# Sums of two MLPs: an accumulating DMA in place of VectorE's adds in the middle blocks

## The chip, the cores and the metric

The kernel runs on one core of a Trainium2 chip. The metric is the device time of one execution in microseconds, here a median of three runs. The core has five engines with a queue of instructions each: TensorE (PE in the rows, its weight loads PEld), VectorE (DVE), ScalarE (ACT), GpSimd (POOL) and SyncE (SP). They wait for each other by semaphores. DMAs are issued from the queues of SP, ACT or POOL.

## The reference

The input is a decaying linear attention over 2 sequences of 768 tokens with 8 heads of 64, followed by two MLPs without residuals, all in float32:

```
x = attention(q, k, v, lam)                       # 1536 tokens x 512
h = x @ w_in          # 512 x 2048
x = (h * clip(h + 3, 0, 6) / 6) @ w_out           # first MLP, 2048 x 512
h = x @ w_in2
out = maximum(0.01 * h, h) @ w_out2               # second MLP
```

The attention goes block by block of 64 tokens, with a state of 64 x 64 per head that decays from block to block.

## The kernel before

The kernel has three stages that overlap at their borders. The attention takes about the first 50 us. Then the two MLPs follow. Every float32 operand of a large product is split into a high and a low part, and a product is taken as three matmuls (high by high, high by low, low by high). TensorE does them in groups of 128 x 512 outputs.

The 2048 hidden units are cut into 16 slices of 128, called f. The 1536 tokens are cut into three tiles of 512, called t. A step is one (f, t): a first-stage product (`gemm1`, 12 matmuls into PSUM), a gate on ScalarE and VectorE that ends in G, and a second-stage product (`gemm2`) of four groups e = 0 to 3, three matmuls each, one PSUM bank per group. The slices are taken in blocks (`BLOCKS`, line 30: 1, 3, 4, 4, 4 slices in the first MLP and four times 4 in the second). Within a block, tile by tile, the groups of all its slices accumulate in PSUM; at the end of a block and tile the four accumulators are added to `sums` in SBUF (`SUM[t][:, e, :]`) and their banks are free for the next tile. In the second MLP the first-stage products of tiles 0 and 1 are taken together by a Strassen scheme (`product`, `keep`, `join`) at two places of each block; tile 2 uses `gemm1`.

The banks are `acc0` to `acc3`. In the first MLP the groups e = 0 and 1 of tile 1 use banks of the pool `a` (`acc_bank`, line 505), so e = 2 and e = 3 always come back to the same banks.

`collect` (line 527) empties an accumulator. In the first block of an MLP (b = 0) ScalarE copies it to `sums`; in every other block VectorE adds it to `sums`. `second` (line 631) registers the four groups of a step and, in the last step of a block and tile, their collects.

Weights come as 64-bit floats in halves of 512 KB, by DMA from SP into a ring of four `raw` buffers (`sizes`, line 120). ScalarE and VectorE convert each half (two activations, two tensor_scalar instructions, two that compose the bits) and split it into high and low parts in a ring of six slots `w`. A raw buffer is free when its bits are composed; in the second MLP one raw buffer of each pair of slices is reused for Strassen's sums of weights and is held longer.

The order of all instructions on every engine is written out ahead by a planner, the class `Order`. Each operation has an engine and a duration, a due time, the operations that it follows, and buffers that it takes and gives back. `issue` runs through a simulated time: whenever an engine is idle, the ready operation with the earliest due time whose buffers are free starts on it, and at that moment its instructions are emitted. The chip then runs each engine's instructions strictly in this order, with waits by semaphores. In the plan a VectorE collect lasts 0.69 us and a ScalarE collect 0.58 us; a bank is given back when the collect ends. The second-stage groups keep their order among themselves (`prev2`), so do the first-stage products (`prev1`).

Of the kernel before, what the change touches and what calls it, by code (L numbers as in the profile page):

```python
# [9 lines left out]
F32 = mybir.dt.float32  # L10
# [4 lines left out]
ALU = mybir.AluOpType  # L15
# [8 lines left out]
P = 128  # L24
TT = 512
# [4 lines left out]
BLOCKS = ((1, 3, 4, 4, 4), (4, 4, 4, 4))  # L30
# [5 lines left out]
T_FIRST, T_STEP, T_COLLECT, HOP = 40.0, 5.45, 2.0, 0.3  # L36
# [6 lines left out]
class Order:  # L43
# [7 lines left out]
    def add(self, engines, fn, due=1e9, after=(), takes=(), frees=()):  # L51


        engines = [engines] if isinstance(engines, tuple) else engines
        self.ops.append((engines, fn, due, [a for a in after if a is not None], list(takes), list(frees)))
        return len(self.ops) - 1
# [59 lines left out]
def decay_attention_two_mlps(ctx: ExitStack, tc: tile.TileContext, qkk, vv, lam, w1, w2, out):  # L116
    nc = tc.nc
    eng = {"act": nc.scalar, "dve": nc.vector, "pool": nc.gpsimd}

    sizes = {"raw": 4, "cv": 3, "cl": 2, "w": 6, "G": 3, "u": 3, "h": 2, "a": 2, "r": 3, "vs": 3}  # L120
    late = {"s": 2, "Gx": 3, "ux": 3}
    const = ctx.enter_context(tc.tile_pool(name="const", bufs=1))
    sb_att = ExitStack()
    pool = {n: (sb_att if n in ("r", "vs") else ctx).enter_context(
                tc.tile_pool(name=n, bufs=sizes[n], **({"space": PSUM} if n in "ha" else {})))
            for n in sizes}
# [5 lines left out]
    add = od.add  # L132

    def new(n, shape, dtype, name=None):
        return pool[n].tile(shape, dtype, tag=name or n, name=name or n)
# [3 lines left out]
    steps = [(l, b, t, f) for l in range(2) for b in range(len(BLOCKS[l])) for t in range(NTT)  # L139
             for f in range(starts[l][b], starts[l][b + 1])]  # L140
# [9 lines left out]
    due2 = [d + 1.5 * T_STEP for d in due1]  # L150
# [14 lines left out]
    SUM = [sums[:, t * KC * TT:(t + 1) * KC * TT].rearrange("p (k n) -> p k n", k=KC) for t in range(NTT)]  # L165
# [99 lines left out]
    def scores(c):  # L265
        def fn(_):

            ps, qk = PA["s", c], QK[c % NQ]
            for h in range(H):
                for b in range(2):  # L270
                    nc.tensor.matmul(ps[own[b], b, h, :], qk[other[b], 1, h, :], qk[other[b], 0, h, :],  # L271
                                     start=True, stop=True)
        return fn
# [54 lines left out]
    st, copies, masks, dense_ops, att_ops = {}, {-1: []}, [], [op_warm], []  # L328
    for c in range(NSC):
        d, last = due_c[c], c + 1 == NSC  # L330
        ks = [] if last else [add(("pool", 1.05), k_decay(c, b), d,
                                  after=[ld["qk", c], op_const, st.get(c - 2)]) for b in (1, 0)]
        pe = ("pe", 1.15)
        qc = add(("act", 1.2) if c else ("none", 0.0), queries(c), d - 0.5, after=[ld["qk", c]], takes=["pair"])
        s = add(pe, scores(c), d, after=[qc, op_warm])
# [5 lines left out]
        if not last:  # L341
            st[c] = add(pe, state(c), d + 1.3, after=ks + [ld["v", c]] + copies[c - 1] + ([op_rows[c % 2]] if c else []),
                        takes=["a"])
# [30 lines left out]
    def low_bits(h):  # L374
        def fn(_):

            CV[h] = [new("cv", [P, DM], U32, "t"), new("cl", [P, DM], U32, "c")]
            nc.scalar.activation(out=CV[h][1], in_=RAW[h][:, :, 0], func=AF.Copy, scale=2.0 ** -29)  # L378
        return fn
# [15 lines left out]
    def compose(h):  # L395
        def fn(_):
            t, c = CV[h]

            nc.vector.scalar_tensor_tensor(out=t, in0=RAW[h][:, :, 1], scalar=0xC0000000, in1=t,  # L399
                                           op0=ALU.bitwise_and, op1=ALU.bitwise_or)  # L400
            nc.vector.tensor_tensor(out=t, in0=t, in1=c, op=ALU.add)  # L401
        return fn
# [37 lines left out]
    for l in range(2):  # L440
        for f in range(NF):
            for j in range(2):
                h = (l, f, j)
                held = l == 1 and j == 0
                ld_w = add(("dma", 1.45), load_w(h), takes=["raw"])
                a = add(("act", 0.67), low_bits(h), after=[ld_w], takes=["cv", "cl"])
                m = add(("act", 0.67), magnitude(h), after=[ld_w, a])
                x = add(("dve", 0.85), exponent(h), after=[m])
                c = add(("dve", 1.4), compose(h), after=[a, x], frees=["cl"] + ["raw"] * (not (held and f % 2)))
# [13 lines left out]
    PH, U, G, ACC = {}, {}, {}, {}  # L463
# [41 lines left out]
    def acc_bank(s, e):  # L505
        return "a" if e < 2 and steps[s][2] % 2 and not steps[s][0] else f"acc{e}"

    def gemm2(s, e):
        def fn(_):
            l, b, t, f = steps[s]  # L510
            wh, wl = W[l, f]
            gh, gl = G[s]
            first, last = f == starts[l][b], f + 1 == starts[l][b + 1]
            if first:
                n = acc_bank(s, e)
                ACC[e] = new("a", [P, TT], F32) if n == "a" else pool["acc"].tile([P, TT], F32, tag=n, name=n)
            es = slice(e * P, (e + 1) * P)
            if l == 0:
                terms = ((wh[:, 1, es], gh), (wh[:, 1, es], gl), (wl[:, 1, es], gh))
            else:  # L520
                terms = ((gh[:, es], wh[:, 1]), (gh[:, es], wl[:, 1]), (gl[:, es], wh[:, 1]))
            for n, (a, x) in enumerate(terms):
                nc.tensor.matmul(ACC[e], a, x, start=(first and n == 0), stop=(last and n == 2))  # L523
            PA["acc", s, e] = ACC[e]
        return fn

    def collect(s, e):
        def fn(x):
            l, b, t, f = steps[s]
            ps, acc = PA["acc", s, e], SUM[t][:, e, :]  # L530
            if b:
                nc.vector.tensor_tensor(out=acc, in0=ps, in1=acc, op=ALU.add)  # L532
            else:
                nc.scalar.copy(out=acc, in_=ps)
        return fn
# [10 lines left out]
    def store(t, e):  # L546
        c0 = (t * SPT + e) * C

        def fn(_):

            for b in range(B):
                queue = nc.scalar if b and t == NTT - 1 else nc.sync
                queue.dma_start(out=out[b * S + c0:b * S + c0 + C, :], in_=SUM[t][own[b], e, :])
        return fn
# [73 lines left out]
    x2_ready, taken, prev1, prev2, sums_of, last1 = {}, {}, None, None, {}, {}  # L628
    gates = {}

    def second(s, gl, w_frees):
        nonlocal prev2
        l, b, t, f = steps[s]
        first, last = f == starts[l][b], f + 1 == starts[l][b + 1]
        sums = []
        for e in range(4):
            bank = acc_bank(s, e)
            prev2 = add(("pe", 0.68), gemm2(s, e), due2[s], after=[gl, w_ready[l, f, 1], prev2],
                        takes=[bank] if first else [], frees=([] if e < 3 else w_frees))
            if not last:  # L640
                continue
            c = add(("dve", 0.69) if b else ("act", 0.58), collect(s, e), due2[s] + T_COLLECT,
                    after=[prev2, *taken.get((t, e), [])], frees=[bank])
            sums.append(c)
            taken[t, e] = [c]
            if l == 1 and b + 1 == len(BLOCKS[l]):
                add(("dma", 0.75), store(t, e), due2[s], after=[c])
        return sums
# [12 lines left out]
    b = len(BLOCKS[1]) - 1  # L661
    due_p["2", b, 2, NF - 2], due_p["2", b, 2, NF - 1] = at, at + 2.72
    for s in range(n0, NS):
        l, b, t, f = steps[s]
        due1[s], due2[s] = due_p["1", f], due_p["2", b, t, f]

    for s in range(n0):
        l, b, t, f = steps[s]
        last = f + 1 == starts[l][b + 1]
        xs = [x_ready[c] for c in range(t * SPT, (t + 1) * SPT)]  # L670
        g1 = add(("pe", 2.73), gemm1(s), due1[s], after=[w_ready[l, f, 0], prev1] + xs, takes=["h", "G"])
        prev1 = g1
        ua = add(("act", 0.69), gate_a(s), after=[g1], takes=["u"])
        gb = add(("dve", 0.69), gate_b(s), after=[ua], frees=["h"])
        gh = add(("act", 0.63), g_high(s), after=[gb])
        gl = add(("dve", 0.69), g_low(s), after=[gh], frees=["u"])
        sums = second(s, gl, ["G"] + ["w"] * (t == NTT - 1))
        if last and b + 1 == len(BLOCKS[l]):
            sums_of[t], last1[t] = sums, g1
# [30 lines left out]
    for p in range(NF // 2):  # L710
# [19 lines left out]
        for f, t, i, c in ((f1, PAIR[0], 0, c11), (f1, PAIR[1], 3, c12), (f2, PAIR[1], 1, c22)):  # L730
            s, n = s_at[f, t], "G" if t == PAIR[0] else "Gx"
# [4 lines left out]
        s = s_at[f2, PAIR[0]]  # L736
        src = PH[s] = lambda p=p: PA["S", p, 0]
        ua = add(("act", 0.6), (lambda s, src: lambda _: (PH.__setitem__(s, src()), leak(s, None)(_)))(s, src),
                 after=[p4], takes=["u"])
# [4 lines left out]
    for f in range(NF):  # L744
        s = next(s for s in range(n0, NS) if steps[s][2:] == (2, f))
        g1 = add(("pe", 2.73), gemm1(s), due1[s], after=[w_ready[1, f, 0], prev1, split[2, 0], split[2, 2]],
                 takes=["a"])
# [4 lines left out]
    for s in range(n0, NS):  # L752
        gl, n = gate[s]
        second(s, gl, [n] + ["w"] * (steps[s][2] == NTT - 1))
# [40 lines left out]
```

## Time and profile before

| | before |
|---|---|
| median of 3 runs | 575.12 us (573.12 to 575.61) |
| profiled execution | 573.51 us |
| its span | 571.3 us |
| TensorE busy | 557.7 us (98%) |
| VectorE busy | 414.0 us (72%) |
| ScalarE busy | 304.0 us (53%) |
| POOL busy | 28.3 us (5%) |
| mean granted TensorE clock | 0.995 of full |

The span goes from the first to the last instruction of the profiled execution; what lies around it is 2.2 us. A busy time is the sum of an engine's instructions; matmuls overlap by their pipelining, so TensorE's busy time says that it is never without one, not that it is at its peak. A granted clock of 1.00 is 2.4 GHz, one of 0.50 is 1.2 GHz.

### The profile page before, as it was taken

To read this page: it belongs to the slowest core of one execution; us is meant where nothing else is said; L and a number is where in the kernel's file an instruction comes from. 1 tells how busy PE (TensorE), PEld (TensorE's weight loads), DVE (VectorE), ACT (ScalarE), POOL (GpSimd) and SP (SyncE) were. 2 spreads that over 40 slices of the span, in tenths; PEclk is the share of its full clock that TensorE was granted. 3 is DMA by queue.
4 is the path that set the end of the run, shared out by engine and by line. 5 is a ranking of instruction groups with operands and counts; after the bars stand their busy time and mean duration, and the time that the engine had idled before them with its cause. 6 is when DMAs were issued, how large, how long until landed. Compare 5 with 4: busy or idle time off the path is not lost.

```text
span 571.3 us, 8498 instructions
## 1 busy us (share of the span) xinstructions
PE 557.7 (98%) x3396; PEld 462.1 (81%) x3396; DVE 414.0 (72%) x676; ACT 304.0 (53%) x510; POOL 28.3 (5%) x33
## 2 busy tenths in 40 slices
PE   8888999999999999999999999999999999999996
PEld 5877888888888888888888888888888888888885
DVE  8678889998848972698879898479864987653222
ACT  5687875557227532564536667477435653443110
POOL 6561000000000000000000000000000000000000
PEclk9899999999999999999999999999999999999999
DMA  8892333224303230012120114213221121000332
GB/s 332 325 357 99 111 110 111 97 87 149 110 1 108 77 110 1 17 57 74 75 74 1 37 38 141 81 38 111 73 75 37 38 74 38 0 1 1 75 73 73
DMA packets 14536, 49.81 MB, mean 87 GB/s; under 512 B 1698, under 2 KB 1698, under 8 KB 14498
## 3 DMA queue, kind: packets, MB, share of 16 engines
q1 hardware_dynamic: 14176, 48.77, 25.3%
q8 instruction: 26, 0.43, 0.3%
q10 hardware_dynamic: 322, 0.52, 0.3%
q14 instruction: 12, 0.10, 0.1%
HBM read 46.14 MB, written 3.15 MB: 86 GB/s over the span
## 4 chain that ended last, share of the span: by engine, by line
PE 91%; DVE 0%; issue 0%
PE acc L523 42%; PE h L475 23%; PE h L602 11%; PE a L475 8%; PE a L523 4%; PE a L602 2%; PE h L308 1%; PE a L296 1%; DVE sums L532 0%; PE pair L271 0%
## 5 line engine op out<-in xcount | busy, mean ns | idle before, releaser
L482 ACT ACTIVATE u<-h,three 128x512 f32<-128x512 f32 x48 | 33.1, 690 | 79.8 <-PE h L475 79.4
L475 PE MATMUL h<-xh,wh 128*128 128x512 f32 x192 | 74.9, 390 | 0.0
L475 PE MATMUL h<-xl,wh 128*128 128x512 f32 x192 | 74.7, 389 | 0.0
L475 PE MATMUL h<-xh,wl 128*128 128x512 f32 x192 | 74.7, 389 | 0.0
L532 DVE TENSOR_TENSOR sums<-acc,sums 128x512 f32<-128x512 f32 x76 | 50.7, 688 | 19.8 <-PE acc L523 19.8
L523 PE MATMUL acc<-Gh,wh 128*128 128x512 f32 x160 | 62.3, 390 | 0.0
L523 PE MATMUL acc<-Gh,wl 128*128 128x512 f32 x160 | 62.3, 389 | 0.0
L523 PE MATMUL acc<-Gl,wh 128*128 128x512 f32 x160 | 62.2, 389 | 0.0
L486 DVE SCALAR_TENSOR_TENSOR u<-u,h 128x512 f32<-128x512 f32 x48 | 32.9, 685 | 26.8 <-ACT u L482 26.7
L409 ACT CAST wh<-t 128x512 fp32r<-128x512 f32 x64 | 38.9, 618 | 24.2 <-DVE t L401 14.5
L523 PE MATMUL acc<-wh,Gh 128*128 128x512 f32 x128 | 49.8, 389 | 0.0
L523 PE MATMUL acc<-wl,Gh 128*128 128x512 f32 x128 | 49.8, 389 | 0.0
L523 PE MATMUL acc<-wh,Gl 128*128 128x512 f32 x128 | 49.8, 389 | 0.0
L401 DVE CUSTOM_DVE_ANT_0 t<-t,c 128x1024 uint16<-128x1024 uint16 x64 | 45.0, 703 | 2.2
L413 DVE TENSOR_TENSOR wl<-t,wh 128x512 fp32r<-128x512 f32 x64 | 42.9, 686 | 4.0 <-ACT wh L409 3.8
L399 DVE SCALAR_TENSOR_TENSOR t<-raw,t 128x512 uint32<-128x512 uint32 x64 | 44.7, 698 | 1.3
L378 ACT ACTIVATE c<-raw 128x512 uint32<-128x512 uint32 x64 | 42.6, 668 | 5.6 <-DVE t L401 4.6
L382 ACT ACTIVATE t<-raw 128x512 f32<-128x512 f32 x64 | 42.5, 664 | 5.0 <-DVE wl L413 5.0
L502 DVE TENSOR_TENSOR Gl<-u,Gh 128x512 fp32r<-128x512 f32 x24 | 16.6, 690 | 39.1 <-ACT Gh L619 39.0
L475 PEld LDWEIGHTS h<-xh,wh 128*128 128x128 f32 x192 | 36.0, 188 | 7.5
L475 PEld LDWEIGHTS h<-xl,wh 128*128 128x128 f32 x192 | 36.0, 188 | 7.5
L475 PEld LDWEIGHTS h<-xh,wl 128*128 128x128 f32 x192 | 36.0, 188 | 7.5
(128 smaller groups left out, 1120.6 us busy)
## 6 DMA issues: line engine op xcount, KB each, us to landing
raw<-w SPq DMA_DIRECT2D x64, 512.0 KB, 3.3
sums<-qkk SPq DMA_DIRECT2D x12, 768.0 KB, 6.8
vs<-vv SPq DMA_DIRECT2D x6, 512.0 KB, 5.4
out<-sums SPq DMA_DIRECT2D x20, 128.0 KB, 2.3
out<-sums ACTq DMA_DIRECT2D x4, 128.0 KB, 3.3
lam_sb<-lam ACTq DMA_DIRECT2D x1, 0.0 KB
```

What stands on the lines that cost most here:

```text
L378: nc.scalar.activation(out=CV[h][1], in_=RAW[h][:, :, 0], func=AF.Copy, scale=2.0 ** -29)
L382: return lambda _: nc.scalar.activation(out=CV[h][0].bitcast(F32), in_=RAW[h][:, :, 1].bitcast(F32), func=AF.Abs)
L399: nc.vector.scalar_tensor_tensor(out=t, in0=RAW[h][:, :, 1], scalar=0xC0000000, in1=t, op0=ALU.bitwise_and, op1=ALU.bitwise_or)
L401: nc.vector.tensor_tensor(out=t, in0=t, in1=c, op=ALU.add)
L409: nc.scalar.copy(out=cut(*h, 0), in_=CV[h][0].bitcast(F32))
L413: return lambda e: eng[e].tensor_tensor(out=cut(*h, 1), in0=CV[h][0].bitcast(F32), in1=cut(*h, 0).bitcast(F32), op=ALU.subtract)
L475: nc.tensor.matmul(ps, a[:, 0, ws], x[:, k, :], start=(n == 0), stop=(n == 3 * KC - 1))
L482: nc.scalar.activation(out=U[s], in_=PH[s], func=AF.Relu, bias=three, scale=1.0)
L486: return lambda _: nc.vector.scalar_tensor_tensor(out=U[s], in0=U[s], scalar=6.0, in1=PH[s], op0=ALU.min, op1=ALU.mult)
L523: nc.tensor.matmul(ACC[e], a, x, start=(first and n == 0), stop=(last and n == 2))
L532: nc.vector.tensor_tensor(out=acc, in0=ps, in1=acc, op=ALU.add)
L602: nc.tensor.matmul(ps, ws[a][:, k * P:(k + 1) * P], xs[b][:, k], start=(i < 3 and n == 0), stop=(n == 5), skip_group_check=True)
```

## The change

In the blocks of an MLP that are neither its first nor its last (`by_dma`), ScalarE copies an accumulator into a staging buffer of a new ring `st` of two buffers, each 128 x 512 float32 (256 KB in all). A DMA issued from POOL with `accum_op=add` then adds the staging buffer to `sums`. The bank is given back when the copy ends; the staging buffer when the DMA ends. For the planner the copy takes 0.58 us of ScalarE and the DMA 3.0 us of POOL. The ring `raw` goes from four buffers to three. The first block's copies and the last block's adds stay as they are.

```diff
-    sizes = {"raw": 4, "cv": 3, "cl": 2, "w": 6, ...}
+    sizes = {"raw": 3, "st": 2, "cv": 3, "cl": 2, "w": 6, ...}
...
+    STAGE = {}
+    by_dma = lambda s: 0 < steps[s][1] < len(BLOCKS[steps[s][0]]) - 1
+
+    def add_up(s, e):
+        t = steps[s][2]
+        return lambda _: nc.gpsimd.dma_start(out=SUM[t][:, e, :], in_=STAGE[t, e], accum_op=ALU.add)
+
     def collect(s, e):
         def fn(x):
             l, b, t, f = steps[s]
             ps, acc = PA["acc", s, e], SUM[t][:, e, :]
-            if b:
+            if by_dma(s):
+                STAGE[t, e] = new("st", [P, TT], F32)
+                nc.scalar.copy(out=STAGE[t, e], in_=ps)
+            elif b:
                 nc.vector.tensor_tensor(out=acc, in0=ps, in1=acc, op=ALU.add)
             else:
                 nc.scalar.copy(out=acc, in_=ps)
...
-            c = add(("dve", 0.69) if b else ("act", 0.58), collect(s, e), due2[s] + T_COLLECT,
-                    after=[prev2, *taken.get((t, e), [])], frees=[bank])
+            far = by_dma(s)
+            c = add(("dve", 0.69) if b and not far else ("act", 0.58), collect(s, e), due2[s] + T_COLLECT,
+                    after=[prev2, *(taken.get((t, e), []) if not far else [])], frees=[bank], takes=["st"] * far)
+            if far:
+                c = add(("pool", 3.0), add_up(s, e), due2[s] + T_COLLECT, after=[c, *taken.get((t, e), [])],
+                        frees=["st"])
             sums.append(c)
             taken[t, e] = [c]
```

## Rows read from the trace of the kernel before

**Rows 1.** The page, parts 1 and 4: busy us and share; chain by engine.
```profile
PE 557.7 (98%) x3396; PEld 462.1 (81%) x3396; DVE 414.0 (72%) x676; ACT 304.0 (53%) x510; POOL 28.3 (5%) x33
...
PE 91%; DVE 0%; issue 0%
```

**Rows 2.** Windows: busy us of PE, PEld, DVE, ACT, POOL; PEclk, DMA share.
```profile
0.00:50.00 50.00, 41.43 (x984) 34.82 (x985) 39.81 (x54) 34.02 (x59) 28.27 (x33) 0.97 0.82 307
50.00:560.00 510.00, 510.00 (x2387) 422.39 (x2386) 370.78 (x618) 269.46 (x452) 0.00 (x0) 1.00 0.20 66
560.00:571.30 11.30, 6.24 (x28) 4.84 (x26) 3.42 (x5) 0.56 (x2) 0.00 (x0) 0.89 0.29 93
```

**Rows 3.** Groups by line and form, the collects: busy us, mean ns.
```profile
L532 DVE TENSOR_TENSOR sums<-acc,sums 128x512 f32<-128x512 f32 x76 | 50.7, 688 | 19.8 <-PE acc L523 19.8
...
L534 ACT COPY sums<-acc 128x512 f32<-128x512 f32 x22 | 12.7, 589 | 0.8
```

**Rows 4.** Chain in order of time, first MLP: start us, us, what.
```profile
87.52 2.72 PE acc L523 x12
90.24 2.72 PE h L475 x12
92.96 1.36 PE a L523 x6
94.32 1.36 PE acc L523 x6
...
188.16 5.44 PE acc L523 x24
```

**Rows 5.** Timeline of TensorE, second MLP: start us, us, line, op, out<-in.
```profile
409.68 0.39 PE L523 MATMUL acc<-wh,Gh 128*128 128x512 f32 x1
...
410.13 0.39 PE L523 MATMUL acc<-wh,Gl 128*128 128x512 f32 x1
...
415.12 0.39 PE L523 MATMUL acc<-wh,Gxh 128*128 128x512 f32 x1
```

**Rows 6.** Timeline of VectorE at the same end of a block.
```profile
409.20 2.73 DVE L532 TENSOR_TENSOR sums<-acc,sums 128x512 f32<-128x512 f32 x4 [0.23 <-PE acc L523]
```

**Rows 7.** Timelines of ScalarE and VectorE and the chain: one gate.
```profile
148.84 0.63 ACT L492 ACTIVATE Gh<-u 128x512 fp32r<-128x512 f32 x1 [0.25 <-DVE u L486]
...
150.65 0.68 DVE L499 SCALAR_TENSOR_TENSOR Gl<-u,Gh 128x512 fp32r<-128x512 f32 x1
...
152.80 1.36 PE a L523 x6
```

**Rows 8.** The page, part 6: issues by queue, KB each, median us to landing.
```profile
raw<-w SPq DMA_DIRECT2D x64, 512.0 KB, 3.3
...
out<-sums SPq DMA_DIRECT2D x20, 128.0 KB, 2.3
```

**Rows 9.** Tiles raw (all, then from 130 us) and out: issue ns, landing us.
```profile
L371 SPq DMA_DIRECT2D raw<-w x64: 327/328/1323, 27.2 to 475.6; - x64
...
DMA to landing us min/median/max: 3.0/3.3/9.4
...
DMA to landing us min/median/max: 3.0/3.3/5.1
...
DMA to landing us min/median/max: 2.2/2.4/4.0
```

**Rows 10.** Timelines of POOL and VectorE; tile raw on VectorE, ns min/median/max.
```profile
40.17 2.52 POOL L261 TENSOR_TENSOR kd<-sums,decay 64x512 f32<-64x512 f32 x2 [1.90 <-issue]
...
40.51 1.27 DVE L399 SCALAR_TENSOR_TENSOR t<-raw,t 128x512 uint32<-128x512 uint32 x1
...
L399 DVE SCALAR_TENSOR_TENSOR t<-raw,t x64: 681/692/1268, 40.5 to 499.1; 128x512 uint32<-128x512 uint32 x64
```

**Rows 11.** SP's weight load and ScalarE's reading of another, early.
```profile
59.05 0.33 SPq L371 DMA_DIRECT2D raw<-w  x1
...
65.20 0.67 ACT L378 ACTIVATE c<-raw 128x512 uint32<-128x512 uint32 x1
```

More of the change, by code (lines that the diff above doesn't have):

```diff
@@ L118, in decay_attention_two_mlps @@
     eng = {"act": nc.scalar, "dve": nc.vector, "pool": nc.gpsimd}
-    sizes = {"raw": 4, "cv": 3, "cl": 2, "w": 6, "G": 3, "u": 3, "h": 2, "a": 2, "r": 3, "vs": 3}
+    sizes = {"raw": 3, "st": 2, "cv": 3, "cl": 2, "w": 6, "G": 3, "u": 3, "h": 2, "a": 2, "r": 3, "vs": 3}
     late = {"s": 2, "Gx": 3, "ux": 3}
```

## The prediction

> **What bounds the kernel now.** I read the page's busy shares first, then its chain, then the work by stage, then the order of the work at a block's end. The shares give TensorE 557.7 of 571.3 us [rows 1], and the chain that ended last is 91% TensorE with VectorE at 0%. A share is a mean over stages, so the windows decide. From 50 to 560 us TensorE is busy 510.00 of 510.00 us at the full granted clock; it is idle 50.00 - 41.43 = 8.57 us in the attention stage and 5.06 us in the last window [rows 2]. VectorE is busy 370.78 us of that long middle stretch, so 139 us of it are idle and TensorE never waits. The reader is to see that every microsecond the change can take from VectorE in the middle is already hidden, and that every microsecond in which TensorE then has to wait is added to the end.
>
> **What moves.** The blocks with 0 < b < last are blocks 1 to 3 of the first MLP and 1 to 2 of the second, with three token tiles each: 15 block ends, 60 accumulators. VectorE loses 60 adds of 0.688 us [rows 3], 41.3 us: worth nothing on the path, by the windows above. ScalarE gains 60 copies of 0.589 us [rows 3], 35.3 us on top of the 269.46 busy in the 510 us: it has room. POOL, idle after 50 us [rows 2], issues 60 DMAs. The last block of each MLP, and so the end of the kernel, stays with VectorE. Each DMA is long done before the next write of the same sums, a whole block of the schedule later. What can cost is the time until a PSUM bank is free: before, one VectorE add frees it; after, the copy does, and the copy needs one of two staging buffers, which comes free only when the DMA two copies earlier has landed.
>
> **When the banks are wanted.** At the end of a block the four groups follow each other at 0.68 us. Take T as the end of the first group, e=0. Between a closing group and the next one on its bank there is usually one first-stage product of 2.72 us: the closing step at 87.52, the product at 90.24, the next step from 92.96, whose e=2 and e=3 come at 94.32 [rows 4]. So a bank is wanted 4.76 us after its group ends. In the second MLP it is the same for e=2: the closing group begins at 409.68 and ends 0.68 later at 410.36, and the next begins at 415.12 [rows 5], 4.76 later. VectorE's adds follow the groups closely there, the first at 409.20 with T = 409.00 [rows 6]. I count 11 ends of this kind (7 in the first MLP, 4 in the second). Two ends have no product between, as in the run of two steps at 188.16 [rows 4]: there a bank is wanted 2.04 us after its group. The last two ends are followed by Strassen products, which don't use these banks, and have ample time.
>
> **When the copies can run.** With X for the time from the copy's end and hop until the DMA has landed: copy e=0 ends at T+0.2+0.6, its DMA goes at T+0.9 and lands at T+0.9+X. Copy e=1 is 0.68 later, its DMA lands at T+1.6+X. Copy e=2 needs the first buffer, so its bank is free at T+0.9+X+0.6; wanted at T+1.36+4.76 = T+6.1. TensorE waits X-4.6 if that is positive. Copy e=3 frees its bank 0.7 later and is wanted 0.68 later, so it adds nothing unless the DMAs are slower one after the other than 0.7 us apart. At the two tight ends the wait is X-1.9, if the order stays as it is.
>
> **X from rows.** No row shows a DMA from POOL, nor an accumulating one. Below, the quickest landing of a 128 KB store is 2.2 us [rows 9]; above, the slowest landing of a weight load is 9.4 us [rows 9]. A plain load of 512 KB lands in 3.3 us at the median [rows 8, 9]; the accumulating DMA moves 256 KB but must read the source and the old sums, 512 KB of reads, so I take 3.3 and add the issue. SP takes 0.33 us for one [rows 9]; the larger work that POOL shows takes 1.26 us, two in 2.52 [rows 10]; I take 0.7, between the two. X = 4.0, an estimate from these rows.
>
> VectorE and POOL do get in each other's way: beside POOL's two products of keys from 40.17 on, the weight instruction at 40.51 took 1.27 us, where its median is 0.692 [rows 10]. If a DMA's issue on POOL lost as much to VectorE, 0.6 us, X would be 4.6, the cover gone, and with the weight loads' 0.9 on top the sum 4.3 us in place of 1.4: 579.4 us. I count this into the first rival, which is why it has a third of the chance. The Trainium skill has a rule on this, on its page "SBUF — State Buffer", section "Who interferes with whom": VectorE and GpSimd share a pair of SBUF ports, an instruction of VectorE in a two-port mode locks GpSimd out until it ends, and so DMAs issued from GpSimd can stall where others can't. The rows above agree that the two share something; whether it reaches a DMA's issue no run here shows yet.
>
> These rows speak of other queues; the Trainium skill speaks of this one. Its page "DMA: Bandwidth & Descriptors", section "Anatomy of one DMA — SWDGE (gpsimd) path", gives about 2.0 us fixed plus the bytes by 436 GB/s; for 256 KB that is 2.6 us, an estimate from the page, and no run here shows it. By it X-4.6 is negative and the sum is the time before; it says nothing of the read of the destination. That is the forecast's outcome, so it has no chance of its own among the rivals.
>
> **The sum.** At X = 4.0 the 11 ordinary ends cost 0: 0.6 us is left. When a weight load is in flight the DMA shares the engines: 64 loads of 3.3 us [rows 9] are 211 of 571 us, 0.37 of the time, so of 13 exposed ends 4.8 meet one. I give those 0.9 us more (between 0 and the 1.8 by which loads themselves differ most after 130 us, 3.3 against 5.1 [rows 9]): X = 4.9, 0.3 us each, 1.4 us. The two tight ends cost 0 to 2 x 2.1 = 4.2 us; I take 0, since the planner counts 3.0 us for each DMA, one after the other, and so cannot write an order in which e=2 is wanted at T+3.4; it puts another first-stage product in. By its own count it frees e=3 at about T+7.5 against T+6.8; it then starts the next product there also, as it does already where two come together. If it can't, that is up to 0.7 us at 11 ends, 7.7 us; I take 0.
>
> **ScalarE's queue.** While ScalarE waits for a staging buffer, gate and weight instructions stand behind it. By the plan copy e=2 comes up at T+3.9; at X = 4.0 it waits to T+4.9, 1.0 us. The gate's chain has Gh at 148.84, Gl at 150.65 and done at 151.33, and the step that reads it at 152.80 [rows 7]: 1.5 us of cover. At X above 4.5 this cover is gone too, but the same wait then already stands in TensorE for the bank, so it is not added.
>
> **Raw buffers 4 to 3.** After the change each weight load waits for the buffer of three loads before. The tightest early case: the sixth load would go at 59.05 in place of the seventh [rows 11], lands 3.3 later at 62.4, and is read at 65.20 [rows 11]. 2.8 us are left, so 0. In the second MLP one raw buffer is held by the Strassen sums at times and two are left; the six converted weight slots hide it. If they don't, eight loads late by 3.3 us would be 26 us.
>
> Against the profiled execution's 573.51 us: 573.5 + 1.4 = 574.9. The median of the runs is 575.12, 1.6 above it; the forecast is 575.1 + 1.4 = 576.5 us.
>
> **Rivals.** (1) *The staging buffers become the bound.* The DMA takes long (two streams into the adder, issue on POOL held up by VectorE, a DMA from POOL slower than one from SP). At X = 6 an ordinary end costs 1.4 us, and 13 ends 18 us: 593 us. It decides from X = 4.6, and from 4.6 + 2.9 / 13 = 4.82 it is visible. For it: no row shows such a DMA, and 0.6 us is a thin cover, and VectorE and POOL share something [rows 10]. Against: the 3.3 us landings. Chance 0.33. (2) *The four DMAs of an end queue behind each other.* If each takes 2 us of the engines or of POOL, e=1 lands 2 us after e=0 and not 0.7, and e=3 costs 2 us more: 3.4 x 13 = 44 us, 619 us. Against it: loads of 512 KB land in 3.0 us at best. Chance 0.08. (3) *Three raw buffers are too few.* 26 us by the sum above at most, half of it 588 us. Against it: the cover of 2.8 us. Chance 0.06. (4) *VectorE's relief shortens the path.* Only the first 50 us have idle TensorE, 8.57 us, and there the change moves only weight loads and the order; a third of it would be 572 us. Chance 0.05.
>
> **Chances and range.** The forecast, no difference that can be seen (about 0.5%, 2.9 us, is what a measurement of this kernel can tell from none), has 0.48. Slower by over 0.5% has rivals 1 to 3, 0.47; faster has 0.05. The likeliest case alone spans 573.5 to 578. The range goes from 573, below which lies rival 4, to 600, which is X = 6.5 at 13 ends; above lie rival 2 and the worst of rival 1.
>
> **What would show it.** DMA issues on POOL with the landing X: under 4.6 us the forecast stands, above it the stall X-4.6 must show as TensorE idle before the e=2 matmuls of the second stage, put down to ScalarE, and ScalarE idle before its staging copies, put down to the DMA. VectorE busy must fall by about 41 us to 373, ScalarE's rise by about 35 to 339. TensorE's 510 us without a gap must stay. The prediction is wrong if gaps appear there with X under 4.6 (order or cover), or if the windows before 50 us change by over 3 us.

## The result and the profile after

The changed kernel took 577.47 us (median of 7 runs, 576.18 to 579.96), the kernel before beside it 573.55 us (7 runs, 572.21 to 575.61): a ratio of 1.0078 [1.0053, 1.0103]. The medians are 3.9 us apart, the ratio makes it 4.5. The forecast was 1.4 us more, inside what can be told from nothing; what came is small but visible, about three times that. That the forecast time, 576.5 us, lies only 1.0 us below the measured one is luck: it stood on the 575.12 us of three runs, and from the 573.55 of seven the same 1.4 us lead to 574.95. The profiled execution took 577.46 us with a span of 575.7 (before 573.51 and 571.3).

The page of the changed kernel, parts 1, 3, 4 and 6, against [rows 1] and [rows 8]:
```profile
PE 559.3 (97%) x3396; PEld 461.8 (80%) x3396; DVE 376.2 (65%) x616; ACT 333.4 (58%) x570; POOL 82.2 (14%) x93
...
q1 hardware_dynamic: 14176, 48.77, 25.4%
q0 software_dynamic: 8640, 15.73, 16.2%
...
PE 72%; issue 12%; DMA 3%; POOL 2%; DVE 1%; ACT 1%; POOLq 0%; ACTq 0%
...
raw<-w SPq DMA_DIRECT2D x64, 512.0 KB, 3.3
...
sums<-st POOLq DMA_DIRECT2D x60, 256.0 KB, 3.7
```
The work moved as computed: VectorE 414.0 to 376.2 us (373 forecast), ScalarE 304.0 to 333.4 (339 forecast; on ScalarE an instruction starts up to 0.1 us before the end of the one ahead, as at 94.63 behind the copy that lasts from 94.14 to 94.73, so 60 copies add 29.4 us and not 35.3). The chain is now 72% TensorE where it was 91% [rows 1]: it leaves TensorE for the new DMAs. TensorE's busy time barely moved, so the shares of a chain don't say how much was lost. The windows do, against [rows 2] (columns as there, the last one GB/s):
```profile
0.00:50.00 50.00, 42.65 (x989) 35.80 (x990) 40.02 (x53) 34.95 (x61) 28.78 (x33) 0.97 0.79 297
50.00:560.00 510.00, 506.82 (x2367) 418.12 (x2366) 332.81 (x559) 297.34 (x508) 53.42 (x60) 1.00 0.39 97
560.00:575.70 15.70, 9.88 (x44) 7.86 (x42) 3.42 (x5) 1.09 (x2) 0.00 (x0) 0.91 0.22 68
```
The middle was full, 510.00 of 510.00; now 3.18 us of it are empty, at the full granted clock. From the changed kernel's waits (us in total, times, longest us) one reads who made them:
```profile
ACT st L540 <- DMA sums<-st: 32.4, 17, 3.5
...
PE acc L523 <- ACT st L540: 2.6, 4, 1.5
...
PE acc L523 <- DVE Gl L499: 0.5, 1, 0.5
```
ScalarE waits 17 times for a landing, 32.4 us together, and most of that is hidden: TensorE stops only five times, 3.2 us in all, four times for a staging copy, once for a gate. All five are in the first MLP; after 225 us none follows.

By the starts of the matmuls (0.227 us apart when nothing waits) the stops delay TensorE by 1.69 us at 94.78, 0.51 at 111.76, 0.69 at 133.21, 0.34 at 194.68 and 0.73 at 220.72, 3.96 together; the matmul after each also comes some 0.1 us late. From the first second-stage product to the last matmul it is 507.00 us before and 511.71 after: +4.7. From the start of the last matmul to the end it is 5.5 before, 6.2 after: +0.7. The first second-stage product came 1.07 us earlier than before; in the thirteen traces of this study, whose attention stage differs in the raw ring and in one tiny DMA alone, that start lies anywhere from 55.9 to 59.7 us, so nothing ties it to the change. 4.7 + 0.7 - 1.07 = 4.3, which is 575.7 - 571.3 but for their rounding. What lies around the span is 1.8 us here and 2.2 before, so the two executions differ by 3.95 us.

### The profile page after: what moved, and what is told of

Its sections match the earlier page's. It is cut to its first block, busy times and chain, and to the rows that moved or that the text cites. A ratio compares the mean times of both kernels' runs of the same rounds, so it can differ in the third digit from the quotient of the medians.

```text
span 575.7 us, 8697 instructions
## 1 busy us (share of the span) xinstructions
PE 559.3 (97%) x3396; PEld 461.8 (80%) x3396; DVE 376.2 (65%) x616; ACT 333.4 (58%) x570; POOL 82.2 (14%) x93
## 3 DMA queue, kind: packets, MB, share of 16 engines
q1 hardware_dynamic: 14176, 48.77, 25.4%
q0 software_dynamic: 8640, 15.73, 16.2%
## 4 chain that ended last, share of the span: by engine, by line
PE 72%; issue 12%; DMA 3%; POOL 2%; DVE 1%; ACT 1%; POOLq 0%; ACTq 0%
PE acc L523 34%; PE h L475 14%; PE h L612 11%; PE a L475 8%; DMA sums<-st 3%; PE a L523 2%; POOL sums L532 2%; PE a L612 2%; PE h L308 1%; ACT st L540 1%; PE a L296 1%; PE pair L271 0%; DVE u L486 0%; DVE t L399 0%; DVE Gl L499 0%
## 5 line engine op out<-in xcount | busy, mean ns | idle before, releaser
L532 POOL DMA_DIRECT2D sums<-st x60 | 53.4, 937 | 421.7 <-ACT st L540 414.1
L540 ACT COPY st<-acc 128x512 f32<-128x512 f32 x54 | 31.7, 587 | 43.3 <-DMA sums<-st 32.4
L399 DVE SCALAR_TENSOR_TENSOR t<-raw,t 128x512 uint32<-128x512 uint32 x64 | 44.1, 689 | 1.3
```

Source lines behind the costliest of these rows:

```text
L532: return lambda _: nc.gpsimd.dma_start(out=SUM[t][:, e, :], in_=STAGE[t, e], accum_op=ALU.add)
L540: nc.scalar.copy(out=STAGE[t, e], in_=ps)
```

## The experiments

Times are medians with the ratio to the kernel before, run beside each; spans, starts and landings are of each profiled execution. "Dense stretch" is from the first second-stage product to the last matmul, "tail" is from the start of the last matmul to the end of the span. Lines of an edit that are not shown are marked by "...".

**e1_raw3: the raw ring alone, on the kernel before.**
```
-    sizes = {"raw": 4, "cv": 3, ...}
+    sizes = {"raw": 3, "cv": 3, ...}
```


> Only the ring of raw weight buffers goes from four to three; every add stays on VectorE. Theory S (TensorE waits for banks because the staging copies wait for the DMA to land): no difference, ratio 0.998 to 1.002, no TensorE gap after 62 us. Rival R (three raw buffers make weights late): 1.005 or more, with gaps in the first MLP where the weights are made.

572.34 us, 0.9996 [0.9974, 1.0017]. Its window of the middle (columns as in rows 2):
```profile
60.00:560.00 500.00, 500.00 (x2208) 414.01 (x2207) 360.78 (x602) 259.24 (x433) 0.00 (x0) 1.00 0.20 66
```
No gap, so three raw buffers by themselves cost nothing and the third rival falls.

**e2_second: the DMA only in the second MLP (24 of the 60).**
```
-    by_dma = lambda s: 0 < steps[s][1] < len(BLOCKS[steps[s][0]]) - 1
+    by_dma = lambda s: steps[s][0] == 1 and 0 < steps[s][1] < len(BLOCKS[1]) - 1
```


> The staged copies and accumulating DMAs only in the second MLP's blocks 1 and 2 (24 of 60); three raw buffers. The changed kernel had no TensorE gap after 225 us, so theory S: no difference, ratio 0.998 to 1.002. A theory that each of these DMAs costs the path something wherever it stands: 24/60 of 0.8%, 1.003.

573.72 us, 1.0022 [1.0005, 1.0039]. The ratio does not tell 1.002 from 1.003; the trace does: the dense stretch is 507.0 without a gap, and what is left is the tail, 6.2. The first MLP alone loses time in the middle.

**e3_early: the changed kernel with one tiny accumulating DMA from POOL at the end of attention**, to see whether the long first landing is that of a queue used for the first time.
```
...
+    def first_dma(_):
+        nc.gpsimd.memset(early, 0.0)
+        nc.gpsimd.dma_start(out=early[:, 0], in_=early[:, 1], accum_op=ALU.add)
+    add(("pool", 3.0), first_dma, due_c[-1], after=ks_last)
...
```


> As the changed kernel, but POOL issues one tiny accumulating DMA at the end of the attention, before the first block end. If the 6.0 and 7.7 us of the first two landings are the first use of this kind of DMA, the first landing drops to 3.3 to 4.6 us and the 1.7 us gap at 95 us goes: 1.5 us faster than the changed kernel, ratio to the kernel before about 1.005. If they are the weight loads in flight, it stays as it was: 1.008.

577.44 us, 1.0091 [1.0064, 1.0118]. The first landings are 5.9 and 7.7 us again, the first gap 1.62 us at 94.80. Not the first use, then; that idea fell. What is in flight with them was left, and e10_load tests it.

**e4_pooladd: POOL adds the staged copy itself, no DMA.**
```
-        return lambda _: nc.gpsimd.dma_start(out=SUM[t][:, e, :], in_=STAGE[t, e], accum_op=ALU.add)
+        return lambda _: nc.gpsimd.tensor_tensor(out=SUM[t][:, e, :], in0=SUM[t][:, e, :], in1=STAGE[t, e], op=ALU.add)
```


> Same order and same two staging buffers, but POOL adds the staging buffer to the sums itself instead of a DMA, about 1.3 us in place of a landing of 3.3 to 7.7. Theory S: no copy waits and the gaps go, ratio 0.998 to 1.002. If the order that the planner wrote is the cost: 1.005 to 1.008 as with the DMA. If POOL and VectorE hold each other up: VectorE's two-input instructions beside it grow from 0.69 to 1.2 us, which its idle time hides, at most 1.003.

586.8 us, 1.0246 [1.0219, 1.0273]: a miss. Timelines of POOL and VectorE in this kernel at its first block end (start us, us, engine, line, op, out<-in):
```profile
87.08 3.47 POOL L532 TENSOR_TENSOR sums<-sums,st 128x512 f32<-128x512 f32 x2 [40.35 <-ACT st L540]
...
87.72 1.68 DVE L401 CUSTOM_DVE_ANT_0 t<-t,c 128x1024 uint16<-128x1024 uint16 x1
89.32 1.79 DVE L499 SCALAR_TENSOR_TENSOR Gl<-u,Gh 128x512 fp32r<-128x512 f32 x1
91.03 0.41 DVE L388 TENSOR_SCALAR t<-t 128x512 f32<-128x512 f32 x1
91.48 1.40 DVE L391 TENSOR_SCALAR t<-t 128x512 uint32<-128x512 uint32 x1
```
A POOL add takes 1.42 us at the mean. Beside 29 of the 60 a VectorE instruction is 0.5 to 1.1 us longer than in the changed kernel: here 0.69 becomes 1.68 and 1.79, and 0.43 becomes 1.40. Gates are written late, and TensorE waits for Gl five times, 6.2 us in all, besides 2.5 us for staging copies and 1.7 us for one operand of the second MLP: the dense stretch is 521.36. The effect of [rows 10] is real, but what it does to VectorE belongs to POOL's arithmetic. In the changed kernel, where POOL only issues DMAs, L399 takes 691 ns at the median and 694 at most after 60 us. An issue takes 0.86 us alone. The second issue of an end, right behind the first, takes 0.89 to 1.13 us in eleven ends and 1.11 to 1.43 in the four where VectorE's tensor_scalar instructions (L388, L391) run beside it. So a hold-up of the issue by some 0.2 to 0.3 us is possible and not shown; the first issues ahead of TensorE's stops have none of these beside them. The Trainium skill's rule that the prediction weighed (page "SBUF — State Buffer", section "Who interferes with whom") agrees with this run in that one of the two engines can hold up the other; here it was VectorE that waited.

**e5_half: of each end's four accumulators two by DMA, two by VectorE**, so no copy waits for a buffer within an end.
```
-            if by_dma(s):
+            if by_dma(s) and e < 2:
...
-            far = by_dma(s)
+            far = by_dma(s) and e < 2
```


> Only the groups e = 0 and 1 of a block end go through the staging buffers and the DMA; VectorE adds e = 2 and 3 as before. No copy then follows another within 3.3 us on its buffer, so no copy waits for a landing, while 30 of the 60 accumulating DMAs and their traffic stay. Theory S (the wait for the staging buffer is the cost): no TensorE gap, ratio 0.998 to 1.002. A theory that the DMAs cost by their traffic (weights late) or by their issue on POOL: half of the 0.8%, 1.004.

573.25 us, 1.0003 [0.9983, 1.0022]. Window of the middle:
```profile
60.00:560.00 500.00, 500.00 (x2207) 414.01 (x2207) 343.38 (x575) 277.58 (x465) 26.45 (x30) 1.00 0.30 82
```
Thirty DMAs are issued, landing in 3.3 to 6.3 us, and TensorE has no gap. No copy waits for a landing either. A long landing costs nothing where nobody waits for its buffer: the price is the wait for the staging buffer, not the DMA's traffic.

**e6_st1: one staging buffer in place of two.**
```
-    sizes = {"raw": 3, "st": 2, ...}
+    sizes = {"raw": 3, "st": 1, ...}
```


> One staging buffer in place of two, so that copies e = 1, 2 and 3 each wait for the landing before. Theory S: bank e = 3 is free some 13.4 us after T (0.8 + 3 x 4.2) and wanted at T + 6.8, less one first-stage product of 2.7 that the planner may pull in: 4 to 6.6 us at 13 ends, 50 to 86 us, ratio 1.09 to 1.15. If the staging wait were not the cost: under 1.015.

657.27 us, 1.1461 [1.1407, 1.1515]. Its waits:
```profile
ACT st L540 <- DMA sums<-st: 91.1, 43, 5.8
...
PE acc L523 <- ACT st L540: 54.6, 24, 4.3
```
The same two links grow from 32.4 and 2.6 us to 91.1 and 54.6; part of the loss is matmuls at a lower clock (mean granted clock 0.946).

**e7_st4: four staging buffers, paid for with one raw buffer.**
```
-    sizes = {"raw": 3, "st": 2, ...}
+    sizes = {"raw": 2, "st": 4, ...}
```


> Four staging buffers, paid for with a raw ring of two. No copy of an end waits for another of the same end. Theory S: the gaps put down to the staging copies go; if two raw buffers are still enough, ratio 0.998 to 1.002. With two raw buffers too few, the gaps are others: before the second stage, put down to the weights' last instruction on VectorE, and the ratio is 1.005 to 1.03.

575.31 us, 1.0040 [1.0025, 1.0055]. No copy waits for a DMA, and the four gaps behind copies are gone. Others came, in the gates: 1.78 us at 102.77, and 0.75 and 0.49 near 131. Neither case came as expected: the ratio lies between the two, and no gap is put down to the weights.
```profile
PE a L523 <- DVE Gl L499: 1.6, 1, 1.6
...
PE acc L523 <- ACT Gh L492: 0.6, 1, 0.6
```
Two raw buffers also change the order of weight and gate work, so what delays these gates is not told apart here.

**e8_plan: the planner is told what the trace shows**: POOL is busy 0.9 us with a DMA, the buffer free 2.5 us later, in place of 3.0 us of POOL each, one after the other.
```
-                c = add(("pool", 3.0), add_up(s, e), ..., frees=["st"])
+                c = add(("pool", 0.9), add_up(s, e), ...)
+                c = add(("none", 2.5), nothing, after=[c], frees=["st"])
```


> The same kernel, but the planner is told what the trace shows of a quiet DMA: POOL busy for 0.9 us, the staging buffer free 2.5 us later, several DMAs in flight at once. It then puts copy e = 3 some 2 us earlier into ScalarE's order. Theory S with a part for the order: the gap of 0.7 us at 220.7 us, where the copy stood behind a gate and not behind a DMA, goes, those behind weight loads stay: ratio 1.003 to 1.006. If the order is no part of it: 1.008.

590.24 us, 1.0301 [1.0272, 1.0329]: a miss. Its waits, and TensorE around one of them:
```profile
ACT st L540 <- DMA sums<-st: 44.2, 28, 3.7
...
PE acc L523 <- ACT st L540: 9.2, 7, 2.5
```
```profile
135.52 0.79 PE L523 MATMUL acc<-Gh,wh 128*128 128x512 f32 x1 [2.38 <-ACT st L540]
136.11 0.63 PE L523 MATMUL acc<-Gl,wh 128*128 128x512 f32 x1
136.54 0.63 PE L523 MATMUL acc<-Gh,wl 128*128 128x512 f32 x1
```
Told that a buffer comes back after 3.4 us, the planner asks for the banks sooner, at most ends with no first-stage product between e=2 and e=3. The quiet landings (3.3 and 4.2 us) are still covered, most longer ones are not: TensorE stops seven times, 9.2 us in all. By the starts of the matmuls these stops make 10.4 of the 17.0 us by which the dense stretch grows, and matmuls at a lower clock behind them 4.5 (last section). The stop of 0.73 us at 220.72 is gone, as expected. The 3.0 us in a row were wrong about POOL and right for the schedule: they were slack.

**e9_plan49: the same with 4.0 us in place of 2.5.**
```
+                c = add(("none", 4.0), nothing, after=[c], frees=["st"])
```


> The whole change, with the planner told 0.9 us of POOL and 4.0 us more until the staging buffer is free, DMAs in flight at once (the run before told it 0.9 and 2.5 and lost 3.0%). If the slack that the planner leaves before a bank is wanted decides: it believes bank e = 2 free only after T + 6.4 and puts another first-stage product ahead of it, so landings up to some 7 us are covered; gaps only at the first ends, where landings reach 7.7 us: ratio 1.000 to 1.004. If a truer count of parallel DMAs is what hurt: slower than 1.01 again.

575.65 us, 1.0050 [1.0032, 1.0068]. That is a little above the 1.004 expected, and one of the two gaps that are left (0.71 at 96.88, 0.82 at 195.98) is not at the first ends. The dense stretch is 509.03 and the tail 6.2. Planned at 3.4 the stretch is +17.0, planned at 4.9 it is +2.0: the slack against the landing decides.

**e10_load: e2_second, where no end stalls, with a plain 512 KB DMA** from ScalarE's queue right behind copy e=0 of each of its six block ends. It writes rows of the output that the real stores overwrite later.
```
...
+            if far and e == 0:
+                add(("act", 0.55), other_load(b, t), due2[s] + T_COLLECT, after=[c])
```


> As the kernel with the change in the second MLP alone (1.002, no TensorE gap, most landings 3.3 us), plus one plain 512 KB DMA, from and to device memory, issued by ScalarE right after the first staging copy of each of the six block ends; it feeds nothing that is kept. If transfers in flight are what makes an accumulating DMA land late: the first landings of each end rise from 3.3 to between 4.3 and 7.7 us, as beside the weight loads of the first MLP, and gaps put down to the staging copies appear at up to four ends, 0.3 to 2 us each, 1 to 6 us in all. If the first MLP's landings were late for another cause: 3.3 us as before and no gap.

577.59 us, 1.0075 [1.0056, 1.0094]. The first end's first landing, 3.4 us in e2_second, is now:
```profile
DMA to landing us min/median/max: 5.6/5.6/5.6
```
and ScalarE and TensorE show there:
```profile
416.75 0.58 ACT L545 COPY st<-acc 128x512 f32<-128x512 f32 x1 [4.28 <-DMA sums<-st]
...
417.39 0.50 PE L523 MATMUL acc<-wh,Gxh 128*128 128x512 f32 x1 [1.22 <-ACT st L545]
```
The six ends' first landings went to 4.2 to 5.6 us, and gaps appeared: 1.38 us at 417.39, 0.36 at 434.23, 1.34 at 482.66, and two below 0.3 before Strassen products, which don't use these banks. At the first end POOL's DMA starts 1.12 us after the end of group e=0, in e2_second 1.13. So one other transfer at the wrong time is enough to make the stall where there was none, at an otherwise unchanged end. That weight loads are that transfer in the first MLP is read from the starts of the loads (next section).

**e11_one: the kernel before with only the tiny DMA of e3_early**, to see whether using POOL's DMA queue at all lengthens the tail.
```
...
+        nc.gpsimd.dma_start(out=early[:, 0], in_=early[:, 1], accum_op=ALU.add)
...
```


> The kernel before with one tiny accumulating DMA from POOL at the end of the attention, and nothing else of the change. Every profile with POOL's DMAs so far ended 6.0 to 6.3 us after the last matmul, every one without 5.4 to 5.6. If the mere use of POOL's DMA queue lengthens the end: 6.0 to 6.3 us here, 0.6 to 0.7 us in all, ratio 1.000 to 1.003. If the many accumulating DMAs do it: 5.4 to 5.6 us. The stretch from the first second-stage matmul to the last stays 507.0 us in both cases.

572.44 us, 0.9993 [0.9978, 1.0007]; dense stretch 507.0, tail 5.5. So the queue's mere use does not lengthen it.

## Why the prediction was right in its mechanism and too small in its cost, point by point

**What held.** VectorE's relief was worth nothing; the raw ring cost nothing (e1_raw3); the issue on POOL did not lengthen VectorE's L399; the two tight ends got their product, with e=2 wanted 6.12 us after T at T = 188.22 and 254.85; the bank waits for the copy and the copy for the landing, as the waits show. The first block end in the changed kernel, POOL, ScalarE and TensorE:
```profile
87.17 1.27 ACT L540 COPY st<-acc 128x512 f32<-128x512 f32 x2
...
88.09 2.16 POOL L532 DMA_DIRECT2D sums<-st  x2 [40.54 <-ACT st L540]
...
92.86 0.39 PE L523 MATMUL a<-Gh,wl 128*128 128x512 f32 x1
...
94.14 0.59 ACT L540 COPY st<-acc 128x512 f32<-128x512 f32 x1 [3.53 <-DMA sums<-st]
...
94.78 0.50 PE L523 MATMUL acc<-Gh,wh 128*128 128x512 f32 x1 [1.53 <-ACT st L540]
```
The matmul was due 0.227 us after 92.86, at 93.09; T is 6.12 before that, 86.97. Copies at 87.17 and on, DMAs from 88.09, the landing, copy e=2 at 94.14, and the matmul 0.64 later. The landing, of the tile in that window:
```profile
DMA to landing us min/median/max: 6.0/6.0/6.0
```
The rule of the prediction, X - 4.6, gives 1.4 us; measured 1.69. What it had too short is the step from the copy to its DMA. The copy starts at T+0.2, as put, and takes 0.59 us, but the DMA starts 0.33 us after it and not 0.1: at T+1.12 in place of T+0.9. With that and 0.1 us more for hops behind the landing (fitted on these ends) the rule gives 1.7. Copies, issues and landings at the two other ends that stalled for a landing:
```profile
105.24 0.66 ACT L382 ACTIVATE t<-raw 128x512 f32<-128x512 f32 x1
105.80 1.06 ACT L540 COPY st<-a 128x512 f32<-128x512 f32 x2
...
106.73 0.86 POOL L532 DMA_DIRECT2D sums<-st  x1 [8.07 <-ACT st L540]
...
DMA to landing us min/median/max: 4.3/4.3/4.3
...
188.41 1.27 ACT L540 COPY st<-acc 128x512 f32<-128x512 f32 x2
...
189.41 0.86 POOL L532 DMA_DIRECT2D sums<-st  x1 [14.04 <-ACT st L540]
...
DMA to landing us min/median/max: 4.6/4.6/4.6
```
The gap at 111.76: T = 105.12, DMA at T+1.61, because ScalarE was still at a weight instruction, X = 4.3, so 0.71 - 0.3 + 0.1 = 0.5, measured 0.51. At 194.68: T = 188.22, DMA at T+1.19, X = 4.6, so 0.4, measured 0.34. At the first end of e10_load: T = 409.89, DMA at T+1.11, X = 5.6, so 1.3, measured 1.38. The mechanism was right to 0.1 us with a longer step from copy to DMA. That step is no matter of these ends alone: fourteen of the fifteen first copies start 0.2 us after T, and no DMA starts before T+1.12.

**"I give those 0.9 us more"** was near in the number of ends and wrong in how the delay is spread. Landings of the tile st over the changed kernel, and of the first of a quiet pair at 167.65:
```profile
DMA to landing us min/median/max: 3.3/3.7/7.7
...
DMA to landing us min/median/max: 3.3/3.3/3.3
```
In quiet X is 3.3, below the 4.0 taken. Four of the fifteen first landings are longer (6.0, 4.3, 4.3 and 4.6 us; 4.8 were forecast), and each has a weight load issued within 0.8 us of its own issue, as the one at 88.56 beside the DMA of 88.09. The eleven others, 3.3 us all, have none within 2.2 us. So a load adds 2.7 us once and 1.0 to 1.3 three times, and up to 3.4 to the second of a pair (7.7, where quiet ones take 4.1 to 4.4), not 0.9 each. Only the 6.0 is clearly above the rule's 4.6, by 1.4 us, which by chance is the whole sum that the prediction had made of 4.8 ends of 0.3. The stops of 0.51 and 0.34 us stand at X = 4.3 and just under 4.6: with the DMA at T+0.9 there would be next to none, and this is the prediction's own sign of a wrong order or cover, a gap with X under 4.6. So three ends stalled, 2.54 us in place of 1.4: 1.4 by the landing, 1.2 by the later DMA and the hops.

The 2.6 us that the prediction estimated from the Trainium skill for this size (page "DMA: Bandwidth & Descriptors", section "Anatomy of one DMA — SWDGE (gpsimd) path") are below even the quiet 3.3; the measurement decides. The loads pay less: the one issued at 88.56 landed in 4.1 us. An accumulating DMA of 256 KB keeps the engines as long as a load of twice its bytes: by part 3 of the profile's page, 16.2% of 575.7 us over 60 is 1.55 us of all 16 engines for each, and the 25.4% for 48.77 MB on q1 make 1.57 us for a load of 512 KB.

**"I take 0"** for the planner's late copy of e=3 failed at one end. The changed kernel's ScalarE and TensorE there:
```profile
217.79 0.59 ACT L540 COPY st<-acc 128x512 f32<-128x512 f32 x1 [2.61 <-DMA sums<-st]
219.50 0.69 ACT L482 ACTIVATE u<-h,three 128x512 f32<-128x512 f32 x1 [1.12 <-PE h L475]
220.09 0.58 ACT L540 COPY st<-acc 128x512 f32<-128x512 f32 x1
...
220.72 0.50 PE L523 MATMUL acc<-Gh,wh 128*128 128x512 f32 x1 [0.57 <-ACT st L540]
```
The last copy waits for no DMA: it is written behind the gate's first step, which waits for a product, and TensorE pays 0.73 us. The prediction had priced this at up to 0.7 for an end and set it to nothing for all 11. In e8_plan and e9_plan49, where the planner writes this copy at another place, the end has no stop.

**"So it is not added"**, on ScalarE's queue, failed once by 0.69 us. In the changed kernel:
```profile
127.88 0.59 ACT L540 COPY st<-acc 128x512 f32<-128x512 f32 x1 [2.04 <-DMA sums<-st]
...
133.21 0.50 PE L523 MATMUL acc<-Gl,wh 128*128 128x512 f32 x1 [0.54 <-DVE Gl L499]
```
ScalarE stands 2.04 us, and VectorE 1.26 us for what ScalarE then writes; from there both run without a pause until a gate comes too late. That the first wait makes the second is read from the order of the work; e7_st4 took the wait away and had late gates too, so it is not shown.

**The tail** was no step of the prediction at all. It is 5.5 to 5.6 us in the kernel before, e1_raw3, e4_pooladd and e11_one, and 6.0 to 6.3 in all nine kernels with 24 or more accumulating DMAs, e5_half and e2_second among them: 0.5 to 0.75 us more than the kernel before, more than the 0.3 between the lowest and the highest of those nine. The last store of the output lands 4.5 us after the start of the last matmul both before and after the change, so the difference lies behind it, in the waits of the engines for each other that close the program. One tiny DMA does not do it. What of the many does stays open.

So at the profile: 2.54 + 0.73 + 0.69 of gaps, 0.5 of late matmuls after them, 0.2 spread in small delays, 0.7 of tail, less the 1.07 of an earlier start. The likeliest case, no visible change, lost by the mechanism that it shares with the first rival, the wait for a staging buffer, at 2.5 us of the 18 that the rival was given: the rival took every exposed end to be long, and only four first landings meet a load.

No kernel here beats the one before. TensorE's 507.0 us without a gap leave VectorE's 41 us nothing to shorten; e5_half, the best form of the change, only equals it.

## What to carry to other kernels

Time taken from an engine that never holds up the bound is worth nothing, while the buffer that the move adds is a new link in the bound's chain: price that link by its landing beside other transfers, not by the quiet median, plus the whole step from the accumulator to the DMA's start (here 1.1 us and more after the group, not 0.9). Let no copy wait for a buffer within one burst (e5_half, which made the burst smaller), and if a planner writes the order, keep its time for the DMA well above the quiet landing: 3.4 us cost 3% here (e8_plan), 4.9 us 0.5% (e9_plan49). An add moved to POOL's arithmetic was paid for on VectorE.

## What was not expected of the hardware

The granted clock fell after a longer stop. In e8_plan TensorE was stopped for 0.58 us before 132.17 and for 2.38 us before 135.52; windows of that kernel (columns as in rows 2; the last three are the granted clock, the DMA share and GB/s):
```profile
135.00:138.00 3.00, 2.48 (x6) 2.00 (x7) 1.44 (x3) 3.00 (x6) 0.88 (x1) 0.51 1.02 244
138.00:141.00 3.00, 3.00 (x14) 2.43 (x13) 2.09 (x4) 1.22 (x3) 0.00 (x0) 0.92 0.67 146
```
0.51 is the lower level, 1.2 GHz, and matmuls start 0.43 us apart there (136.11, 136.54) in place of 0.227. The stop of 1.53 us in the changed kernel did not lower it: the granted clock is 1.00 from 90 to 102 us. Nor did one of 2.20 us at 137.62 in e4_pooladd, with 1.00 from 134 to 146 us; what else decides is not shown here. A stall of this size can therefore cost more than its length, a part of e6_st1's and e8_plan's loss.

An elementwise add on POOL made a VectorE instruction beside it about 1 us longer (e4_pooladd), while with 60 DMA issues on POOL L399 stayed at 694 ns at most after 60 us, as before.
